# Layer norm's root taken for two tiles at once and applied behind the second product, w_out's mean from chunk sums, and one expert fewer turned by TensorE

## The chip, the core and the metric

The program runs on one core of a Trainium2 chip. Its time is device microseconds (us) of one execution. The kernel before takes 569.43 us as the median of 3 runs (568.84 to 570.12); the execution that the profiler recorded took 570.03 us, of which the trace spans 568.3.

## The reference

Three stages follow each other: a linear attention with a decaying state over 4 batches, 8 heads and 768 positions of width 48; a block with two products and a layer norm; and a mixture of 8 experts of which each token goes to one.

```python
h = x @ w_in                                    # 3072x384 @ 384x1024
e = exp(h - max(h)); sm = e / (sum(e) + 1e-9)
solu = h * sm
ln = (solu - mean(solu)) / sqrt(var(solu) + 1e-6) * g_ln
x = ln @ w_out                                  # 1024x384
expert = argmax(x @ w_gate); g = max of softmax(x @ w_gate)
out = g * (relu(x @ w1[expert]) @ w2[expert])
```

## The kernel before

The 3072 tokens are 24 tiles of 128 rows. Every product of precision is made of three fp16 products (high by high, high by low, low by high halves of fp32 numbers).

**Attention**, for each tile i: `kpow`, `rev` and `ktrans` prepare keys and receptances, `scores` multiplies them, `causal` masks them, `ahi` and `alo` split them into fp16 halves, `attend` makes the output, and `update`, `advance` and `decay` move the state on. For the first `NU` tiles the bonus term is made on TensorE by four products of two columns (L489); for later tiles by `ruk`, `asum` and `aval` on GpSimd and VectorE.

**The block**, for each tile: `yhi`, `ylo` and a DMA transpose turn its rows, `mm1` is the first product (18 matmuls of 512 columns), `hmax` its row maximum, `hexp` the exponential, `hsolu` the product with its sum. `hvar` squares on ScalarE. `hse` and `hseed` then make one factor per row from the sum of exponentials and the variance: one small ScalarE step (L583) and five more (L600 to L608), of which the second, a power of -1/2, is GpSimd's. `zscale` and `zlo` scale the rows by this factor into an fp16 high and low half, `ztrans` turns both by a DMA transpose, and `mm2` is the second product (24 matmuls of 392 columns, 384 of output and 8 gate scores, since `w_gate` is folded into `w_out`). For the last two tiles TensorE turns the scaled rows (`zturn`). `choose`, `xrow`, `gexp`, `gate`, `rank`, `place` and `send` pick the expert and send the row to its place in DRAM.

**Preparing w_out** (L238 to L290): it is loaded in four pairs of 128-row chunks, scaled by `g_ln`, extended by the gate's eight columns (`wout_fold`, `wout_gate`) and then freed of its column mean: `wout_mean` (L274) makes the mean with one matmul for each of the eight chunks, `wout_centre` takes it off.

**The experts**: nine parts y (expert 0 in two). `gather` fetches the rows; they are turned either by TensorE (`etrans`, L929) or by two DMA transposes (`eturn`). `EM` is a mask of the parts from y = 2 on that TensorE turns: 60 stands for y = 2, 3, 4, 5. `emm1` and `emm2` are the products, `rhi` and `rlo` split what stands between them, `split` (L832) makes the halves of the weights.

**The order of the work** is made by a planner inside the kernel (`plan`, L1271): each step is an `op` with an engine, a cost and what it comes after, and a table of numbers `X` gives due times. It takes steps one by one and fixes the order of instructions on each engine. Steps marked `either` go to GpSimd or VectorE, as the planner sees fit. Where it sees TensorE idle it puts matmuls of ones that compute nothing (`keep`, L1264), outside of the planned stretch from `K0` to `K1`. Each engine works through its instructions in their order.

Of the kernel before, what the change touches and what calls it, by code (L numbers as in the profile page):

```python
# [17 lines left out]
ALU = mybir.AluOpType  # L18
# [28 lines left out]
SQK = 2.0 / (SZ * 32 * FF)  # L47
GSC = 1.0 / (SW * SZ)
# [4 lines left out]
def body(ctx, tc, rkvs, rs, flat, w, u, w_in, w_out, w1, w2, out):  # L53
# [48 lines left out]
    X = dict(GQ=-1854.59, XA=-53.96, CF=172.95, CT=-2317.0, NF=5, NE=5, EM=60, E2=0, NU=5, QD=3, pr=1, look=-1606.34,
             prod=-4519.04, square=861.08, PK=14, ET=-65.59, GG=-3164.81, SO=-11608.92, FL=-1060.46, OL=1, ybuf=10,
             tmp=1, rkv=3, rT=3, LAT=0.06, SELF=0.05, PRE=0.6, EPS=0.09, TA=340.17, TB=415.99, TM=318.03, NA=8, NB=9,
             M0=1321.55, W0=-891.53, TW=2430.46, W1=-4264.59, TV=-522.72, PF=964.9, PW=1670.76, F0=972.63, EL=3, e=3,
             S0=-214.25, P0=7.7, D0=2.0, L0=-5070.67, L1=1799.29, U0=478.97, KG=-3.83, PT=2, ZT=4046.59, F2=-3101.97,
             TE=22.51, GA=-3791.47, GW=-3748.66, GN=2103.67, DB=1.0, KS=1.22, RD=0.1, RP=0.2, K0=91.31, K1=927.65,
             xtrans=206.21, kev=-3325.25, ahi=-5711.54, vlo=-3049.91, ruk=7806.69, attend=988.22, choose=10050.87,
             xhi=-4754.85, vhi=6188.75, own=7638.3, hvar=1885.43, hmax=-10736.42, gexp=6290.26, ktrans=-11388.48,
             ldr=3880.33, hexp=-1616.58, ztrans=1589.84, asum=8759.56, rev=-3492.12, xlo=239.09, decay=2965.24,  # L110
             alo=6303.56, rank=-1150.26, ld=125.71, xrow=13548.5, mm2=1284.96, causal=596.44, hseed=-5672.49,
             send=-7316.86, hsolu=3051.8, yout=-2009.24, zlo=3420.27, scores=-2533.28, place=-5242.89, WQ=-8553.91,
             advance=2287.51, update=-6787.84, zscale=-1258.1, hroot=-2799.46, mm1=-125.41, aval=6068.5, kpow=-2190.79)
# [19 lines left out]
    g2, low, chk = (const.tile([P, x], F32, name=n) for n, x in (("g2", NG + 6), ("low", NG + 7), ("chk", NCHK)))  # L133
# [71 lines left out]
    raw = {}  # L205

# [89 lines left out]
    def fold_all():  # L296
# [6 lines left out]
        for c in range(0, KF, 2):  # L303
# [7 lines left out]
            wout_gate(c)  # L311
        wout_mean()
# [260 lines left out]
    def hexp(i):  # L573
# [5 lines left out]
        A.activation(e, tk["h", i], AF.Exp, bias=st[:, 0:1], scale=1.0 if i is None else 1.0 / (SY * SI), accum_out=st[:, 1:2])  # L579
# [5 lines left out]
    def hsolu(i):  # L585
# [219 lines left out]
    def stem(key):  # L805
        return stem(key[0]) if isinstance(key, tuple) else key
# [758 lines left out]
```

## Time and profile before

| | |
|---|---|
| median of 3 runs | 569.43 us |
| profiled execution, its span | 570.03 us, 568.3 us |
| TensorE matmul busy | 531.8 us (94%) |
| VectorE busy | 415.3 us (73%) |
| ScalarE busy | 415.7 us (73%) |
| GpSimd busy | 243.1 us (43%) |

Attention and the block run side by side up to about 290 us; the block ends and the experts begin between about 320 and 360 us; the experts run to 554.9 us, and the last rows are written behind that. Shares of busy time are averages over stretches with different limits: a reader should look at the stretch that a change falls in, at whom the engine that sets the pace waits for there, and only then at the cost of one instruction. A matmul of fp32 stands in the trace as two rows.

### The profile page before, as it was taken

To read this page: it belongs to the slowest core of one execution; us is meant where nothing else is said; L and a number is where in the kernel's file an instruction comes from. 1 tells how busy PE (TensorE), PEld (TensorE's weight loads), DVE (VectorE), ACT (ScalarE), POOL (GpSimd) and SP (SyncE) were. 2 spreads that over 40 slices of the span, in tenths; PEclk is the share of its full clock that TensorE was granted. 3 is DMA by queue.
4 is the path that set the end of the run, shared out by engine and by line. 5 is a ranking of instruction groups with operands and counts; after the bars stand their busy time and mean duration, and the time that the engine had idled before them with its cause. 6 is when DMAs were issued, how large, how long until landed. Compare 5 with 4: busy or idle time off the path is not lost.

```text
span 568.3 us, 10629 instructions
## 1 busy us (share of the span) xinstructions
PE 531.8 (94%) x3892; PEld 352.0 (62%) x3892; DVE 415.3 (73%) x667; ACT 415.7 (73%) x898; POOL 243.1 (43%) x250
## 2 busy tenths in 40 slices
PE   3889999999999999999899988999999899999990
PEld 2777675666756676667555556864555455566770
DVE  7998979988779998899868617556777767755110
ACT  4868799998878687868658954988686969687210
POOL 4246733787878788968413131100023303040310
PEclk9999999999999999999899999999999999999995
DMA  7666691685967697742578426666469889882100
GB/s 285 207 191 196 188 254 58 135 180 123 163 184 143 157 196 144 192 122 64 103 190 177 103 70 215 187 191 212 163 166 233 211 215 213 193 246 85 27 24 25
DMA packets 113260, 91.38 MB, mean 161 GB/s; under 512 B 89148, under 2 KB 99350, under 8 KB 112816
## 3 DMA queue, kind: packets, MB, share of 16 engines
q1 hardware_dynamic: 108240, 81.14, 56.2%
q0 software_dynamic: 4960, 9.49, 5.5%
q8 instruction: 32, 0.52, 0.4%
q14 instruction: 28, 0.23, 0.1%
HBM read 57.19 MB, written 12.55 MB: 123 GB/s over the span
## 4 chain that ended last, share of the span: by engine, by line
PE 61%; DVE 16%; DMA 11%; ACT 7%; issue 3%; SPq 1%; POOL 0%; ACTq 0%; DVEq 0%; POOLq 0%
PE emm L949 13%; PE mm L650 10%; PE mm L565 10%; PE emm L992 8%; PE emm L974 7%; DMA xg<-xs 3%; DMA stage<-in_moe_w 3%; PE attend L493 2%; PE scores L459 2%; DMA raw<-in_moe_w_out 2%; PE update L507 2%; PE attend L496 2%; DVE z L615 2%; DVE e L588 1%; PE ktrans L443 1%
## 5 line engine op out<-in xcount | busy, mean ns | idle before, releaser
L1024 POOL DMA_INDIRECT out<-o,gt x29 | 35.1, 1211 | 175.1 <-ACT o L1020 96.2
L650 PE MATMUL mm<-wo,zT 128*128 128x392 f16 x576 | 101.2, 333 | 2.2 <-ACT zT L635 1.1
L949 PE MATMUL emm<-exT,w1h 128*128 128x256 f16 (+8 forms) x432 | 98.7, 317 | 2.5 <-DVE hl L963 2.5
L565 PE MATMUL mm<-wi,xT 128*128 128x512 f16 x432 | 97.2, 379 | 0.3 <-DMA xT<-yy 0.3
L650 PEld LDWEIGHTS <-zT 128*128 128x128 f16 x576 | 55.4, 99 | 40.9 <-issue 1.9
L565 PEld LDWEIGHTS <-xT 128*128 128x128 f16 x432 | 41.3, 98 | 47.5 <-DMA xT<-yy 0.5
L949 PE MATMUL emm<-exT,w1l 128*128 128x256 f16 (+8 forms) x216 | 68.5, 317 | 0.0
L949 PEld LDWEIGHTS <-w1h 128*128 128x128 f16 x432 | 41.7, 97 | 27.3 <-issue 2.9
L963 DVE SCALAR_TENSOR_TENSOR hl<-emm,hh 128x928 f16<-128x928 f32 (+8 forms) x32 | 32.2, 1008 | 30.3 <-ACT hh L960 30.2
L960 ACT ACTIVATE hh<-emm 128x928 f16<-128x928 f32 (+8 forms) x32 | 27.1, 846 | 30.9 <-PE emm L949 14.2
L446 POOL TENSOR_TENSOR rT<-rT,trT 128x512 f32<-128x512 f32 x21 | 30.2, 1441 | 33.5 <-DMA rT<-in_rT 27.9
L841 DVE SCALAR_TENSOR_TENSOR w1l<-stage,w1h 128x1024 f16<-128x1024 f32 x24 | 29.2, 1221 | 18.2 <-ACT w1h L837 17.9
L701 POOL DMA_INDIRECT xs<-row,pos x24 | 28.1, 1172 | 21.7 <-DMA xg<-xs 5.7
L615 DVE SCALAR_TENSOR_TENSOR z<-e,st,z 128x1024 f16<-128x1024 f32 x22 | 34.1, 1551 | 2.1 <-ACT z L611 2.1
L841 DVE SCALAR_TENSOR_TENSOR w2l<-stage,w2h 128x768 f16<-128x768 f32 x32 | 30.0, 951 | 7.5 <-ACT w2h L837 7.2
L571 DVE TENSOR_REDUCE st<-mm 128x1 f32<-128x1024 f32 x24 | 29.2, 1217 | 8.4 <-issue 4.1
L974 PE MATMUL emm<-w2h,hl 128*128 128x384 f16 (+3 forms) x104 | 33.9, 326 | 0.0
L974 PE MATMUL emm<-w2h,hh 128*128 128x384 f16 (+3 forms) x104 | 33.9, 326 | 0.0
L493 PE MATMUL attend<-sdec,rT 128*128 128x96 f32 x160 | 33.9, 296 | 0.0
L974 PE MATMUL emm<-w2l,hh 128*128 128x384 f16 (+3 forms) x104 | 33.9, 326 | 0.0
L992 PE MATMUL emm<-hl,w2h 128*128 128x464 f16 (+3 forms) x96 | 33.0, 344 | 0.0
L992 PE MATMUL emm<-hh,w2l 128*128 128x464 f16 (+3 forms) x96 | 33.0, 344 | 0.0
(256 smaller groups left out, 1357.6 us busy)
## 6 DMA issues: line engine op xcount, KB each, us to landing
rkv<-in_rkv SPq DMA_DIRECT2D x24, 576.0 KB
stage<-in_moe_w SPq DMA_DIRECT2D x16, 768.0 KB
stage<-in_moe_w SPq DMA_DIRECT2D x8, 1024.0 KB
rT<-in_rT SPq DMA_DIRECT2D x24, 256.0 KB
stage<-in_moe_w SPq DMA_DIRECT2D x8, 512.0 KB
raw<-in_moe_w_in SPq DMA_DIRECT2D x3, 1024.0 KB
raw<-in_moe_w_out SPq DMA_DIRECT2D x4, 768.0 KB
xs<-zf SPq DMA_DIRECT2D x8, 337.8 KB
```

The lines of the kernel that those rows point to most:

```text
L446: on[0].tensor_tensor(tk["rT", i], tk["rT", i], trT, op=ALU.mult)
L493: T.matmul(ps[:, j * 96:j * 96 + 96], rT[:, j, :], sdec[:, j].rearrange("p a d -> p (a d)"), start=True, stop=False, skip_group_check=True)
L565: T.matmul(ps[:, n, :], x[a][:, j, :], wi[b][:, j, n * 512:(n + 1) * 512], start=(j == 0 and m == 0), stop=(j == KD - 1 and m == 2))
L571: V.tensor_reduce(st[:, 0:1], tk["h", i], op=ALU.max, axis=AX.X, negate=True)
L615: V.scalar_tensor_tensor(z[:, 1, :], tk.pop(("e", i)), tk["st", i][:, 10:11], z[:, 0, :], op0=ALU.mult, op1=ALU.subtract)
L650: T.matmul(ps[:, 0:OW], zz[:, a, c, :], wo[b][:, c, :], start=(c == 0 and m == 0), stop=(c == KF - 1 and m == 2))
L841: V.scalar_tensor_tensor(lo, d[:, x], (S1, S2)[m - 1], hi, op0=ALU.mult, op1=ALU.subtract)
L949: T.matmul(ps[:, x, :].rearrange("p (j t) -> p j t", t=d["n"]), a[:, j, fc * P:(fc + 1) * P], d["xT"][:, 0:d["nt"], b, j, 0:d["n"]], start ...
L963: V.scalar_tensor_tensor(cols(d, "hl", q), d.pop(("pm", q)), 0.0, cols(d, "hh", q), op0=ALU.max, op1=ALU.subtract)
L974: T.matmul(ps[0:n, 0:DM], a[:, c, j * n:j * n + n], b[:, c, :], start=(c == 0 and m == 0), stop=(c == KF - 1 and m == 2))
L992: T.matmul(ps[:, 0:d["nr"]], a[:, c, m * P:(m + 1) * P], b[:, c, :], start=(c == 0 and x == 0), stop=(c == KF - 1 and x == 2))
L1024: G.indirect_dma_start(out=apart["out"].pop(0), out_offset=bass.IndirectOffsetOnAxis(ap=d["gt"][0:n, j, 1:2].bitcast(U32), axis=0), in_=d. ...
```

## The change

The factor of layer norm is no longer applied to the rows before the second product. `zscale` and `zlo` now multiply by a constant `ZC`, directly behind `hsolu`; `mm2` works on rows without the root, and the root is applied to its results, as the scale of `xrow`, `choose` and `gexp`. `hse` and `hseed` go from the planned part; `hroot` stands in their place: seven small steps on columns of two tiles at once (one ScalarE, four VectorE, two GpSimd; the last two tiles get one each), 13 times in all. `choose` and `xrow` of both tiles of a pair come after it. The two tiles that TensorE turns are turned as they come from `hsolu`, and the constant is applied on the way out of PSUM.

`wosum` adds the pairs of w_out chunks (four pairs, three additions of 128x784 fp32, on GpSimd or VectorE), and the mean is made of the two sums by two matmuls in place of eight.

`EM` is 28 in place of 60: TensorE turns y = 2, 3, 4, and y = 5 goes to the DMA transposes. `NU` and `NE` are 4 in place of 5: tile 4 makes its bonus term on GpSimd and VectorE, and its `aval` and `decay` leave ScalarE. All due times of the table differ, and `K0` is 488 in place of 91, so that `keep` may stand anywhere in the planned program before that. `marks2` checks three more bounds.

```diff
-             tmp=1, rkv=3, rT=3, LAT=0.06, SELF=0.05, PRE=0.6, EPS=0.09, TA=340.17, TB=415.99, TM=318.03, NA=8, NB=9,
+             tmp=1, rkv=3, rT=3, LAT=0.06, SELF=0.05, PRE=0.6, EPS=0.13, TA=423.54, TB=347.88, TM=332.72, NA=8,
...
+    def wout_sum(c, eng=None):
+        (eng or on[0]).tensor_tensor(raw["sum"], raw["sum"] if c > 2 else sto[:, 0:2], sto[:, c:c + 2], op=ALU.add)
...
-        for c in range(KF):
-            T.matmul(ps[:, 0:OW], mmean.to_broadcast([P, P]), sto[:, c, :], start=(c == 0), stop=(c == KF - 1))
+        for c in range(2):
+            T.matmul(ps[:, 0:OW], mmean.to_broadcast([P, P]), raw["sum"][:, c, :], start=(c == 0), stop=(c == 1))
...
+    def hroot(p):
+
+        c = slice(2 * p, 2 * p + 2) if 2 * p < NT - 2 else slice(p + NT // 2 - 1, p + NT // 2)
+        s, m, v, t, y, f, nf = (lv[:, x, c] for x in range(7))
+        A.activation(t, s, AF.Square, scale=1e-3 * ZA, bias=zeps)
+        yield
+        V.scalar_tensor_tensor(t, v, ZA ** 2, t, op0=ALU.mult, op1=ALU.add)
+        yield
+        G.tensor_tensor(y, t, mhalf.to_broadcast([P, c.stop - c.start]), op=ALU.pow)
+        yield
+        G.tensor_tensor(f, y, y, op=ALU.mult)
+        yield
+        V.tensor_tensor(t, t, f, op=ALU.mult)
+        yield
+        V.scalar_tensor_tensor(nf, t, 3.0, y, op0=ALU.subtract, op1=ALU.mult)
+        yield
+        V.tensor_scalar(f, nf, -1.0, None, op0=ALU.mult)
...
-        A.activation(tk["z", i][:, 0, :], tk["e", i], AF.Copy, scale=tk["st", i][:, 10:11])
+        A.activation(ztile(i)[:, 0, :], tk["e", i], AF.Copy, scale=tk["st", i][:, 10:11] if i is None else ZC)
...
-        A.activation(row[:, 0:DM], tk["pz", i][:, 0:DM], AF.Copy, scale=GSC if i is not None else tk["scale"][:, 0:1])
+        A.activation(row[:, 0:DM], tk["pz", i][:, 0:DM], AF.Copy, scale=lv[:, 5, i:i + 1] if i is not None else tk["scale"][:, 0:1])
...
-        op(("hseed", i), "", [("act", .29), ("pool", .58), ("act", .3), ("act", .36), ("act", .3)], [("hvar", i), ("hse", i)], hseed, i, first=f + X["hseed"])
+            op(("hroot", p), "", [("act", .28), ("dve", .17), ("pool", .58), ("pool", .3), ("dve", .17), ("dve", .17), ("dve", .17)], [("hvar", i)] + [("hvar", i - 1)] * (i < NT - 2), hroot, p, first=f + X["hseed"])
```

On TensorE, around the mean of w_out, the order before has two `wout_fold`s apart, eight matmuls of the mean, and a first product behind them (`mm_925` and `mm_1041` are those of tiles 3 and 4):

```order
L565 MATMUL mm_925<-wi_112,xT 128x512
...
L259 MATMUL wout_part<-ident,sto 128x128 x6
L459 MATMUL scores<-rT_143,kT 128x128 x8
L269 MATMUL wout_fold<-few,gT 128x8 x6
L443 MATMUL ktrans<-ident,kp_137 128x128 x4
L278 MATMUL mean<-sto,mmean 128x392 x8
L565 LDWEIGHTS xT
L565 MATMUL mm_1041<-wi_111,xT 128x512
```

The same place now:

```order
L576 MATMUL mm_901<-wi_114,xT 128x512
...
L265 MATMUL wout_part<-ident,sto 128x128 x6
L275 MATMUL wout_fold<-few,gT 128x8 x12
L470 MATMUL scores<-rT_146,kT 128x128 x8
L454 MATMUL ktrans<-ident,kp_140 128x128 x4
L287 MATMUL mean<-sum,mmean 128x392 x2
L576 LDWEIGHTS xT
L576 MATMUL mm_1020<-wi_114,xT 128x512
```

The last folds stand ahead of the scores, and six matmuls of the mean are gone. Between this mean and the first `mm2`, the order before holds the first product of tile 4, the scores of tile 8, seven `keep` and the attention of tile 6; now it holds the first products of tiles 4 and 5, the attention of tiles 6 and 7 and the update of tile 7, and no `keep`.

On TensorE, where the block ends, the order before goes from the second product of tile 23 (`mm_4286`) straight to the turning of the first expert's rows:

```order
L650 LDWEIGHTS zT
L650 MATMUL mm_4286<-wo_113,zT 128x392
L929 MATMUL etrans<-ident,xg 128x128 x6
L684 LDWEIGHTS mask_77
L684 MATMUL rank<-oh,mask_77 128x8
L685 LDWEIGHTS ones_71
L685 MATMUL rank<-cum,ones_71 128x8
L949 LDWEIGHTS w1h
L949 MATMUL emm_4351<-exT,w1h 128x256
```

The same place now:

```order
L678 MATMUL mm_4184<-wo_116,zT 128x392
L712 LDWEIGHTS mask_77
L712 MATMUL rank<-oh,mask_77 128x8
L713 LDWEIGHTS ones_71
L713 MATMUL rank<-cum,ones_71 128x8
L1303 LDWEIGHTS ones_71
L1303 MATMUL keep<-ones_71 128x512
...
L957 MATMUL etrans<-ident,xg 128x128 x6
...
L977 LDWEIGHTS w1h
L977 MATMUL emm_4284<-exT,w1h 128x256
```

Two `keep` stand ahead of the turning and five behind it; twelve more follow ahead of y = 1 and y = 2. Of 43 `keep` in all, 19 stand here and 24 early; before, all 36 stood early.

On VectorE, late in the loop, the steps that make `choose` and the low half for a tile stand before without any step of the root:

```order
L663 MAX mx<-mm_3431 128x8
L670 TENSOR_SCALAR oh<-mm_3431,mx 128x8
L615 SCALAR_TENSOR_TENSOR z<-e,st,z 128x1024
L501 SCALAR_TENSOR_TENSOR av<-attend,av 128x384
L438 SCALAR_TENSOR_TENSOR vl<-rkv_141,vh 128x384
```

The like place now, with the root of tiles 16 and 17 (`lv`):

```order
L617 SCALAR_TENSOR_TENSOR lv<-lv 128x2
L698 TENSOR_SCALAR oh<-mm_3238,mx 128x8
L414 TENSOR_TENSOR kp_140<-rkv_143,tkm 128x8x48
L648 SCALAR_TENSOR_TENSOR z<-e,z 128x1024
L582 TENSOR_REDUCE st<-mm_3295 128x1
L623 TENSOR_TENSOR lv<-lv 128x2
L717 ISA mx,rs<-rank,oh 128x8
L717 ISA rs 128x1
L625 SCALAR_TENSOR_TENSOR lv<-lv 128x2
L627 TENSOR_SCALAR lv<-lv 128x2
```

Between the root's first step on VectorE and its second, in which GpSimd's two fall, four other instructions stand.

## Rows read from the trace of the kernel before

**Rows 1.** Busy time by stretch: length, engines (instructions), granted clock, DMA share, GB/s.
```profile
20.00:60.00 40.00, 38.01 (x306) 31.64 (x306) 37.62 (x50) 31.79 (x81) 19.70 (x15) 0.96 0.60 185
...
200.00:250.00 50.00, 49.40 (x444) 33.90 (x444) 45.43 (x68) 39.19 (x99) 42.18 (x39) 1.00 0.74 164
250.00:300.00 50.00, 47.88 (x390) 30.80 (x390) 41.97 (x66) 34.33 (x87) 25.67 (x25) 0.97 0.50 124
...
450.00:500.00 50.00, 50.00 (x299) 28.91 (x297) 36.41 (x43) 37.06 (x58) 6.24 (x6) 1.00 0.88 214
```

**Rows 2.** Waits of TensorE: whom for, us in total, times, longest.
```profile
PE scores L459 <- ACT kT L450: 4.7, 3, 2.3
PE emm L949 <- DVE hl L963: 2.5, 2, 1.6
...
PE rank L684 <- DVE exT L935: 1.2, 1, 1.2
PE mm L650 <- ACT zT L635: 1.1, 1, 1.1
PE etrans L929 <- DMA xg<-xs: 1.0, 1, 1.0
PE mm L650 <- DVE zT L639: 0.8, 1, 0.8
```

**Rows 3.** Groups of TensorE by shape: count, busy us, mean ns, idle before.
```profile
L1269 PE MATMUL keep<-ones 128*128 128x512 f16 x36 | 10.1, 411 | 0.0
...
L278 PE MATMUL mean<-sto,mmean 128*128 128x392 f32 x16 | 5.4, 492 | 0.0
...
L489 PE MATMUL attend<-uw,pr 128*128 128x2 f32 x40 | 4.9, 245 | 0.0
...
L929 PE MATMUL etrans<-ident,xg 100*128 100x100 f32 x12 | 1.5, 261 | 0.2 <-PE etrans L929 0.2
```

**Rows 4.** TensorE in order of time behind the mean: start, us, count.
```profile
94.04 1.69 PE L1269 MATMUL keep<-ones 128*128 128x512 f16 x7
```

**Rows 5.** TensorE in order of time, end of attention: start, us, count, idle before.
```profile
263.83 4.15 PE L650 MATMUL mm<-wo,zT 128*128 128x392 f16 x24
...
272.18 1.16 PE L459 MATMUL scores<-rT,kT 64*128 64x128 f32 x16 [2.12 <-ACT kT L450]
...
273.34 5.82 PE L650 MATMUL mm<-wo,zT 128*128 128x392 f16 x24
```

**Rows 6.** Groups of ScalarE by shape: small steps of the factor.
```profile
L606 ACT ACTIVATE st<-st,mthree 128x1 f32<-128x1 f32 x24 | 9.1, 377 | 0.1
L604 ACT ACTIVATE st<-st 128x1 f32<-128x1 f32 x24 | 6.9, 289 | 4.0 <-POOL st L602 3.6
...
L583 ACT ACTIVATE st<-st,seps 128x1 f32<-128x1 f32 x24 | 6.7, 285 | 0.1
```

**Rows 7.** Groups of VectorE by shape.
```profile
L615 DVE SCALAR_TENSOR_TENSOR z<-e,st,z 128x1024 f16<-128x1024 f32 x22 | 34.1, 1551 | 2.1 <-ACT z L611 2.1
...
L475 DVE TENSOR_TENSOR al<-AT,ah 128x1024 f16<-128x1024 f32 x8 | 14.2, 1772 | 2.5 <-ACT ah L471 2.5
...
L282 DVE TENSOR_TENSOR sto<-mean,sto 128x784 f32<-128x784 f32 x4 | 3.7, 966 | 1.1 <-PE mean L278 1.1
...
L344 DVE TENSOR_TENSOR tt<-tt 128x4 f32<-128x4 f32 x6 | 1.0, 167 | 0.2
```

**Rows 8.** Groups of GpSimd by shape.
```profile
L475 POOL TENSOR_TENSOR al<-AT,ah 128x1024 f16<-128x1024 f32 x11 | 24.1, 2190 | 6.0 <-ACT ah L471 5.8
...
L602 POOL TENSOR_TENSOR st<-st,mhalf 128x1 f32<-128x1 f32 x24 | 18.7, 779 | 32.7 <-ACT st L600 32.7
```

**Rows 9.** GpSimd and VectorE at 68 us, and VectorE at 79, in order of time.
```profile
67.90 2.13 POOL L475 TENSOR_TENSOR al<-AT,ah 128x1024 f16<-128x1024 f32 x1 [0.37 <-ACT ah L471]
...
67.95 2.50 DVE L534 SCALAR_TENSOR_TENSOR yy<-av,yy 128x384 f16<-128x384 f32 x1
...
78.64 0.55 DVE L534 SCALAR_TENSOR_TENSOR yy<-av,yy 128x384 f16<-128x384 f32 x1
```

More of the change, by code (lines that the diff above doesn't have):

```diff
@@ L100, in body @@
+    for t, x in ((mhalf, -0.5), (mthree, -3.0), (seps, 1e-12 * SQK), (zeps, 1e-12 * ZA), (geps, 1e-9 * SX * S1 * S2), (mmean, -1.0 / FF)):
         V.memset(t, x)
-    X = dict(GQ=-1854.59, XA=-53.96, CF=172.95, CT=-2317.0, NF=5, NE=5, EM=60, E2=0, NU=5, QD=3, pr=1, look=-1606.34,
-             prod=-4519.04, square=861.08, PK=14, ET=-65.59, GG=-3164.81, SO=-11608.92, FL=-1060.46, OL=1, ybuf=10,
-             tmp=1, rkv=3, rT=3, LAT=0.06, SELF=0.05, PRE=0.6, EPS=0.09, TA=340.17, TB=415.99, TM=318.03, NA=8, NB=9,
[L105 to L113, printed above, removed]
@@ new lines, in body @@
+    X = dict(wosum=-1635.67, GQ=-616.8, XA=1394.41, CF=-290.97, CT=-6359.1, NF=5, NE=4, EM=28, E2=0, NU=4, QD=3, pr=1,
+             look=-2341.52, prod=-6524.65, square=2604.7, PK=14, ET=528.66, GG=-3384.61, SO=-18943.02, FL=-798.97, OL=1,
+             ybuf=10, tmp=1, rkv=3, rT=3, LAT=0.06, SELF=0.05, PRE=0.6, EPS=0.13, TA=423.54, TB=347.88, TM=332.72, NA=8,
+             NB=9, M0=845.85, W0=-2374.1, TW=2832.34, W1=-4662.95, TV=-874.11, PF=-1936.1, PW=4107.56, F0=1220.97, EL=3,
+             e=3, S0=-1054.86, P0=7.7, D0=2.0, L0=-6821.53, L1=5887.81, U0=-1599.74, KG=-8.84, PT=2, ZT=820.97,
+             F2=-3035.94, TE=132.85, GA=-5551.93, GW=-3010.05, GN=7245.56, DB=1.13, KS=1.34, RD=0.1, RP=0.2, K0=488.46,
+             K1=1255.14, xtrans=-2101.6, kev=-5486.82, ahi=-6274.18, vlo=779.5, ruk=17058.24, attend=940.63,
+             choose=11798.2, xhi=-6359.67, vhi=3018.11, own=6575.55, hvar=3502.44, hmax=-16082.56, gexp=7779.16,
+             ktrans=-8999.85, ldr=1692.18, hexp=2493.89, ztrans=-1764.42, asum=2142.54, rev=-3671.2, xlo=1537.36,
+             decay=4482.54, alo=6355.85, rank=1187.18, ld=-663.05, xrow=9507.73, mm2=1410.61, causal=926.75,
+             hseed=-12404.97, send=-11051.31, hsolu=2227.53, yout=1363.01, zlo=8166.78, scores=-1290.24, place=-8047.87,
+             WQ=-4668.31, advance=500.44, update=-7582.49, zscale=-5085.08, hroot=490.76, mm1=111.97, aval=14450.14,
+             kpow=-530.85)
@@ L126, in fold_pools @@
         sto = cv.tile([P, KF, OW], F32, name="sto", bufs=1)
+        raw["sum"] = cv.tile([P, 2, OW], F32, name="sum", bufs=1)
         return cv, sto
@@ L132, in body @@
     hacc = const.tile([P, 4 * (E + 1)], F32, name="hacc")
-    g2, low, chk = (const.tile([P, x], F32, name=n) for n, x in (("g2", NG + 6), ("low", NG + 7), ("chk", NCHK)))
+    lv = const.tile([P, 7, NT], F32, name="lv")
+    g2, low, chk = (const.tile([P, x], F32, name=n) for n, x in (("g2", NG + 6), ("low", NG + 10), ("chk", NCHK)))
     G.memset(hacc, 0.0)
@@ L1157, in body @@
         op(("send", i), "", [("act", .2), ("pool", 1.1), ("none", 4.0)], [("place", i), ("xrow", i), ("gate", i)] + [("fill", e) for e in range(E)], send, i, first=f + X["send"])
+    for i in range(NT):
+        for n in ("choose", "xrow"):
+            ops[n, i]["after"].append(("hroot", i // 2 if i < NT - 2 else i - NT // 2 + 1))
     b_left = set(ops)
```

69 lines of the change are left out of this document (37 added, 32 removed).

## The prediction

> **What bounds the kernel now.** I read the busy time by stretch first. TensorE has 49.40 us of 50 busy in the loop from 200 us on, and all 50.00 of 50 in the experts from 450 us on [rows 1]. The granted clock stands at 1.00 there, so this is work at the full 2.4 GHz and not slow work. In such stretches a matmul that goes is time that goes. Between 20 and 60 us it is different: TensorE's 38.01 of 40 contain most of the 36 `keep` matmuls, 10.1 us in all [rows 3], which compute nothing; VectorE is at 37.62 of 40 with real work and sets the pace [rows 1].
>
> The second view is whom TensorE waits for. Beyond the start it waits little: 4.7 us for ScalarE's `kT`, 2.5 us for VectorE's `hl` in the experts, and where the block ends 1.2, 1.1, 1.0 and 0.8 us, together 4.1 [rows 2]. The third is order of time: of the waits for `kT` one stands at 272 us. It is 2.12 us, and behind it a second product takes 5.82 us in place of 4.15 [rows 5]: TensorE had stood idle, and its clock then fell to the lower level, 1.2 GHz, for a while (0.97 is the granted mean from 250 to 300 us [rows 1]). That is 1.67 us more, 3.8 us for this one stall.
>
> So time can come from four places: TensorE's own work, the stall at 272 us, the waits where the block ends, and the pace of VectorE at the start.
>
> **The change part by part.** I add to the profiled execution's own time, 570.03 us, of which 568.3 is span and 1.73 lies around it; it is 0.60 above the median of the runs.
>
> *The mean of w_out.* Eight fp32 matmuls are 16 rows and 5.4 us; two are four rows. Twelve rows at 5.4/16 = 0.34 go: -4.0 us of TensorE [rows 3]. Three additions of 128x784 come: two on GpSimd and one on VectorE. A like addition on VectorE takes 0.966 [rows 7]; on GpSimd the nearest is the 128x1024 subtract of 2.19 [rows 8], and I take 2 each. The last one stands between the last `wout_fold` and the mean. It is covered by the scores and `ktrans` that the order now puts there, and by VectorE, which has five operations to do before it can take the mean off; uncovered it would cost its 2 us.
>
> *Tile 4's bonus term.* Four products of two columns go, 8 of 40 rows in 4.9 us: -1.0 us [rows 3].
>
> *What the start takes back.* These 5.0 us go where VectorE sets the pace. If it alone decided when `mm2` may begin, all 5.0 would come back as waiting; if not, none. VectorE does not get less to do there: it loses two preparations of tile 1 and the bonus of tile 4, and gains an addition, four small root steps and an earlier `zlo`. But the order brings work forward: before the first `mm2` it now has a first product, an attention and an update more and no `keep`, where seven `keep` of 1.69 us stood [rows 4]. That work would otherwise stand in the full stretch behind, so the saving is kept if TensorE is fed. I take +1.0, nearer to the end of nothing lost.
>
> *The factor.* Per tile ScalarE loses five small steps, four of 285 to 289 ns and one of 377, about 1.52 us [rows 6], 36.6 in all, and gets one step per root. TensorE does not see this in full stretches: ScalarE is not the bound there (39.19 of 50 [rows 1]). It does matter at 272 us, where `kT` came late from ScalarE. Fewer steps in front of it make that wait shorter; but it was late because VectorE was, and VectorE has no less to do. The ends are 0 and -3.8 (wait and slow clock gone); I take -1.5.
>
> VectorE gets four root steps in each of 13 roots at about 0.167 [rows 7]: 8.7 us. Five of the `alo` subtracts (1.772 each [rows 7], 8.9 us) go from VectorE to GpSimd. By count the two cancel. The root's steps on VectorE wait for GpSimd's power (0.779 [rows 8]) and its square, and in order behind the waiting step stand `place`, the next `hmax` and `hsolu`, for which the first product's PSUM bank and then `mm2` wait. Four other instructions stand between, the low half and a row maximum among them, longer than power and square together. So 0; without this cover each root could hold VectorE for those two and a subtract in front of them on GpSimd (the rival below).
>
> `choose` and `xrow` now wait for the root of the pair, so the first tile of a pair keeps its PSUM bank about a tile longer. Behind `xrow` on ScalarE stand the gate's steps and the next exponential. The order puts the root's ScalarE step ahead of them, and nobody needs the sent row before the gather: 0. It could cost a wait for a bank; I see none from this in the trace of before and put its worst into the range.
>
> *The moved subtracts.* A subtract on GpSimd is not free for VectorE. At 67.95 us a split of 384 columns took 2.50 us beside a GpSimd subtract of 2.13 that had begun 0.05 earlier; at 79 us the same shape took 0.55 [rows 9]. So five moved subtracts give VectorE between 8.9 us (nothing beside them suffers) and -0.9 us (each holds up such a split by 1.95). The Trainium skill, "SBUF — State Buffer", section "Who interferes with whom", says that VectorE instructions with two SBUF inputs and GpSimd instructions that read SBUF lock each other out for a whole instruction; this row agrees. By that rule the relief of VectorE is nearer to the second end, and the sum stays as it is, since TensorE is the bound, but the slower rival gets nearer.
>
> *Expert part y = 5.* Twelve transposes of 100 columns go from TensorE: -1.5 us [rows 3], in a stretch where it has 50.00 of 50. Two DMA transposes come, in SP's queue ahead of the last two loads of expert 4's weights, with the share of the DMA engines at most 0.88 [rows 1]. Those weights are needed two products of other rows later, so 0; if the queue ran late, TensorE would wait for them. The orders of the products differ there too; the 2.5 us of waits for `hl` may go or double, and I take 0.
>
> *Where the block ends.* The waits of 4.1 us come from the last two tiles' long way through factor, scaling and turning, and from the gathers. That way is shorter by the factor and one scaling pass. But 19 `keep` stand here now, and they run whether the wait is there or not: 19 x 1.69/7 = 4.6 us [rows 4]. Best case they just fill what was waiting, +0.5; worst they come on top, +4.6. I take +1.0.
>
> *The three checks* stand ahead of the last products on a VectorE with nothing else to do: 0.
>
> Sum: -4.0 - 1.0 + 1.0 - 1.5 - 1.5 + 1.0 = -6.0, so 564.0 for a profiled execution like that of before, and 563.4 from the median of 569.43. I forecast 563.8.
>
> **The rivals.**
>
> *More is gained.* The stall at 272 us goes wholly (-3.8 in place of -1.5), the waits for `hl` go (-2.5), and the start takes nothing back (-1.0): 563.8 - 5.8 = 558.0. For it: ScalarE is relieved by 33 us, and the loop's full stretches leave it idle. Against it: VectorE was at the root of the stall.
>
> *The start eats its savings.* VectorE sets the pace to the mean and beyond, the 5.0 us come back as waits, the stall stays: 570.03 - 1.5 + 1.0 = 569.5, no change. For it: 37.62 of 40 [rows 1]. Against it: the work that is brought forward.
>
> *VectorE becomes the bound of the loop (slower).* Its idle time is 4.6 us of 50 at 200 us [rows 1]. Two roots fall into 50 us. Each could hold it for a subtract, a power and a square on GpSimd, at most 2.19 + 0.78 + 0.78 = 3.75, so 7.5, and 1.3 for their own steps. The moved subtracts give back at most 8.9 over some 190 us of loop, 2.3 per 50. That is 7.5 + 1.3 - 2.3 - 4.6 = 1.9 lost per 50 us, 7.2 over 190. The savings inside this part are then no savings, only the 1.5 of the experts remain: 570.03 + 7.2 - 1.5 = 575.7. It decides from the point where a root holds VectorE for (4.6 + 2.3 - 1.3)/2 = 2.8 us; if the moved subtracts give nothing back, from 1.65. Against it: the four instructions in between.
>
> *The `keep` are pure cost.* The waits at the block's end stay and 4.6 us come on top: 563.8 + 3.6 = 567.4.
>
> **How the numbers follow.** The forecast (561 to 567) gets 0.48, more gained 0.15, the start eats its savings 0.12, VectorE the bound 0.15, `keep` pure cost 0.10. A change under 0.2% of 569.43, 1.1 us, is about what a measurement of this kernel can't tell from none. Faster: 0.48 + 0.15, most of the 0.10, and a little of the third case, 0.72. Same: most of the third, 0.11. Slower: 0.17, the fourth with a tail of waits for banks and weights. The range is to leave out 2 in 10: from 558.0, the better case, to 571.5, which is past the third case and reaches into the slower one. The forecast's own range is 561 to 567.
>
> **What would show it right or wrong.** Right: four rows of the mean, about 1.3 us; the first `mm2` at most 2 us later than before, with a first product and an attention more in front of it; no wait of 2 us for `kT`; `etrans` without the 100-column shape; idle time of TensorE at the block's end under 2 us with 19 `keep` in it. Wrong: a wait of TensorE for the mean or for `wo`; VectorE idle before L623 for POOL by more than 1.65 us a root; TensorE's share in the loop below 98%; a gap before expert 4's second product for its weights.

## The result, and the profile after

The changed kernel takes 562.66 us (median of 4 runs, 561.07 to 562.90) beside 569.36 of the kernel before: ratio 0.9881, 95% interval 0.9841 to 0.9922. Measured once more beside the kernel before (e5 below) it was 0.9843 (0.9795 to 0.9892). So it is faster, by 6.7 us in the first pair of medians; the forecast was 563.8. Some executions of a kernel run some per cent longer at a lower granted clock: the ratios here leave them out, the medians and single runs given below do not. The execution of the profile took 562.63 us with a span of 560.9, 7.4 less than before.

| stage of the profile, us | before | after | difference |
|---|---|---|---|
| up to the first `mm2` | 96.54 | 97.00 | +0.46 |
| first `mm2` to the end of the last | 243.13 | 235.99 | -7.14 |
| to the first expert product | 2.11 | 2.37 | +0.26 |
| expert products | 212.96 | 212.19 | -0.77 |
| rest | 13.56 | 13.35 | -0.21 |

The busy times of three of these stages follow, in the columns of [rows 1]: the stage, its length, then TensorE's busy time. Before:

```profile
0.00:96.54 96.54, 83.60 (x655) 63.22 (x656) 85.30 (x140) 75.81 (x168) 46.20 (x63) 0.98 0.64 194
96.54:339.67 243.13, 237.84 (x1929) 154.43 (x1924) 200.44 (x317) 189.40 (x486) 156.97 (x154) 0.99 0.65 146
...
341.78:554.74 212.96, 209.32 (x1311) 133.64 (x1310) 127.50 (x199) 147.78 (x239) 37.86 (x31) 1.00 0.62 173
```

After:

```profile
0.00:97.00 97.00, 85.35 (x664) 64.04 (x665) 86.90 (x145) 74.22 (x150) 56.99 (x71) 0.95 0.70 208
97.00:332.99 235.99, 231.11 (x1887) 151.09 (x1884) 206.38 (x355) 170.58 (x385) 163.11 (x160) 1.00 0.64 144
...
335.36:547.55 212.19, 210.82 (x1311) 133.60 (x1310) 128.71 (x204) 148.27 (x238) 40.40 (x31) 1.00 0.64 177
```

Up to the end of the last `mm2`, TensorE is busy 5.0 us less (321.44 to 316.46) and idle 1.7 us less (18.23 to 16.53). The gain shows behind the first `mm2`, but most of the work that went stood in front of it. Now one more first product (18 matmuls) and one more attention and update stand there (and the scores of one tile fewer), and the first `mm2` is only 0.46 late. By groups the 5.0 us are: the mean -2.5, tile 4's bonus -1.0, twelve `keep` fewer at the start -1.9 (24 in 8.2 us for 36 in 10.1), a second product that ran at the lower clock before -1.7, and rows beside the mean that ran at the lower clock after, +1.8; the rest is small. In the experts idle time fell by 2.3 us and busy time rose by 1.5: twelve `keep` now stand there, and the transposes of y = 5 went.

The waits of TensorE after, to be read beside [rows 2] (whom for, us in total, times, longest):

```profile
PE scores L470 <- ACT kT L461: 3.4, 3, 1.6
PE ktrans L454 <- DVE mx L691: 1.1, 1, 1.1
PE etrans L957 <- ACT o L1008: 1.1, 3, 0.5
PE count L748 <- POOL cum L720: 1.0, 1, 1.0
...
PE emm L977 <- DVE hl L991: 0.3, 1, 0.3
```

The waits of `mm2` for `zT` are gone, those for `hl` fell from 2.5 to 0.3, and new ones of about 1 us came: for VectorE's `mx` and GpSimd's `cum`. The groups that answer to [rows 3]:

```profile
L1303 PE MATMUL keep<-ones 128*128 128x512 f16 x43 | 13.3, 434 | 0.0
...
L500 PE MATMUL attend<-uw,pr 128*128 128x2 f32 x32 | 3.9, 243 | 0.0
...
L287 PE MATMUL mean<-sum,mmean 128*128 128x392 f32 x4 | 2.9, 876 | 0.0
```

The mean has four rows, as said, but one takes 876 ns where it took 492. TensorE in order of time around it shows why (start, us):

```profile
77.25 2.93 PE L275 MATMUL wout_fold<-few,gT 128*128 128x8 f32 x24
80.11 2.08 PE L470 MATMUL scores<-rT,kT 64*128 64x128 f32 x16
82.12 1.11 PE L454 MATMUL ktrans<-ident,kp 128*128 128x128 f32 x4
83.03 2.88 PE L287 MATMUL mean<-sum,mmean 128*128 128x392 f32 x4
85.71 4.44 PE L576 MATMUL mm<-wi,xT 128*128 128x512 f16 x18
```

Behind 24 rows of 8 columns the scores take 2.08 us; elsewhere the same 16 rows take 1.16. The mean granted clock from 60 to 100 us is 0.91, where it was 1.00 before; so for some us it was the lower level, 1.2 GHz. The wait of 2.12 us in [rows 5] stands at the scores of tile 23. There it is gone; the longest wait for `kT` in the loop is now at tile 21:

```profile
251.96 1.16 PE L470 MATMUL scores<-rT,kT 64*128 64x128 f32 x16 [1.64 <-ACT kT L461]
253.06 4.15 PE L678 MATMUL mm<-wo,zT 128*128 128x392 f16 x24
```

It is 1.64 us, and the second product behind it takes 4.15 us and not 5.82: the clock stayed up. At both places ScalarE was not busy with small steps before it made `kT`. It stood idle and waited for VectorE, first before, then after:

```profile
271.15 0.49 ACT L655 ACTIVATE row<-mm 128x384 f32<-128x384 f32 x1 [2.76 <-DVE oh L670]
```

```profile
250.37 1.06 ACT L482 ACTIVATE ah<-AT 128x1024 f16<-128x1024 f32 x1 [2.67 <-DVE AT L478]
```

In both cases `kT` is ScalarE's next instruction.

VectorE's root steps are dearer than the 0.167 us taken from [rows 7]:

```profile
L617 DVE SCALAR_TENSOR_TENSOR lv<-lv 128x2 f32<-128x2 f32 x11 | 4.6, 420 | 0.2 <-ACT lv L615 0.2
...
L623 DVE TENSOR_TENSOR lv<-lv 128x2 f32<-128x2 f32 x11 | 4.2, 381 | 1.3 <-POOL lv L621 1.3
...
L627 DVE TENSOR_SCALAR lv<-lv 128x2 f32<-128x2 f32 x11 | 3.4, 307 | 0.3
L625 DVE SCALAR_TENSOR_TENSOR lv<-lv 128x2 f32<-128x2 f32 x11 | 3.2, 287 | 0.3
```

### The profile page after: what moved, and what is told of

It is laid out like the page before. It is cut to its first block, busy times and chain, and to the rows that moved or that the text cites. A ratio compares the mean times of both kernels' runs of the same rounds, so it can differ in the third digit from the quotient of the medians.

```text
span 560.9 us, 10536 instructions
## 1 busy us (share of the span) xinstructions
PE 529.7 (94%) x3867; PEld 350.1 (62%) x3867; DVE 424.2 (76%) x718; ACT 396.0 (71%) x780; POOL 263.2 (47%) x265
## 4 chain that ended last, share of the span: by engine, by line
PE 68%; DVE 13%; ACT 6%; DMA 5%; issue 5%; POOL 1%; SPq 0%; ACTq 0%; DVEq 0%; POOLq 0%
PE emm L977 16%; PE mm L678 12%; PE mm L576 11%; PE emm L1020 8%; PE emm L1002 7%; PE scores L470 3%; PE attend L504 2%; PE attend L507 2%; PE update L518 2%; DMA rkv<-in_rkv 2%; DVE yy L545 1%; DMA stage<-in_moe_w 1%; DMA xg<-xs 1%; DMA raw<-in_moe_w_out 1%; DVE vl L449 1%
## 5 line engine op out<-in xcount | busy, mean ns | idle before, releaser
L1052 POOL DMA_INDIRECT out<-o,gt x29 | 37.7, 1299 | 171.6 <-ACT o L1048 97.4
L678 PE MATMUL mm<-wo,zT 128*128 128x392 f16 x576 | 99.3, 329 | 0.5 <-ACT kT L461 0.5
L486 POOL TENSOR_TENSOR al<-AT,ah 128x1024 f16<-128x1024 f32 x16 | 37.0, 2311 | 7.1 <-ACT ah L482 6.9
L457 POOL TENSOR_TENSOR rT<-rT,trT 128x512 f32<-128x512 f32 x21 | 28.6, 1362 | 21.0 <-DMA rT<-in_rT 16.5
L414 POOL TENSOR_TENSOR kp<-rkv,tkm 128x384 f32<-128x384 f32 x23 | 25.1, 1093 | 18.7 <-DMA rkv<-in_rkv 14.8
L648 DVE SCALAR_TENSOR_TENSOR z<-e,z 128x1024 f16<-128x1024 f32 x22 | 33.2, 1509 | 0.3 <-ACT z L609 0.3
L470 PE MATMUL scores<-rT,kT 64*128 64x128 f32 x384 | 29.4, 296 | 4.2 <-ACT kT L461 3.4
```

The costliest lines, as they stand in the source:

```text
L470: T.matmul(ps[:, a, j * P:(j + 1) * P], kT[h, j, :], rT[h, j, :], start=True, stop=True)
L486: on[0].tensor_tensor(al, tk.pop(("at", i)), tk["ah", i], op=ALU.subtract)
L648: V.scalar_tensor_tensor(z[:, 1, :], tk.pop(("e", i)), tk["st", i][:, 10:11] if i is None else ZC, z[:, 0, :], op0=ALU.mult, op1=ALU.subtract)
L678: T.matmul(ps[:, 0:OW], zz[:, a, c, :], wo[b][:, c, :], start=(c == 0 and m == 0), stop=(c == KF - 1 and m == 2))
L1052: G.indirect_dma_start(out=apart["out"].pop(0), out_offset=bass.IndirectOffsetOnAxis(ap=d["gt"][0:n, j, 1:2].bitcast(U32), axis=0), in_=d. ...
```

## The experiments

All are compared with the kernel before on the chip of their own runs. Its medians there were 569.59 us (e1 to e4), 571.84 (e5 to e8) and 571.13 (e9 to e12), its single runs 565 to 581, and the intervals are some 0.3 to 0.7% to either side. The changed kernel itself stands at 0.988 and 0.984; an edit of it is judged against these two. It ran on the chip of e6 and e7, and not on those of e1 to e4 and e9 to e12. "Same order" means that the planner's numbers are left alone, so the instructions keep their places.

**e5, the changed kernel again.** No edit.

> The changed kernel itself once more, beside the kernel before on the chip of these runs, as the measure for the kernels that differ from it by one edit. Expected ratio to the kernel before 0.988, within the interval of the first measurement, some 563. If the clock falls at chance places from run to run, the single runs spread over some us, and a profile can show the lower clock in another place than at 78 to 86 us.

0.9843 (0.9795 to 0.9892), 562.33 us, runs from 561.41 to 563.74. Its span of 559.7 has the slow stretch too, in part: scores 2.08, but the mean 1.60, and the first `mm2` at 95.26. So the same instructions meet the lower clock for a longer or shorter time from one execution to the next.

**e1, keep the clock up before the mean.**

```diff
         ps = gTs[c] = sml("wout_fold", slot)
+        if c == KF - 2:
+            for _ in range(7):
+                T.matmul(ps, ones16, ones16.unsqueeze(1).to_broadcast([P, 4, P]), start=True, stop=True)
```

> The changed kernel, in the same order, with seven keep matmuls (128x512) put between the third and the fourth group of wout_fold, where 24 matmuls of 8 columns stand one behind the other and behind which the scores, ktrans, the mean and a first product ran at the lower clock. Theory (TensorE sets the time here, and the changed kernel lost part of the mean's saving to the lower clock): scores 2.08 to 1.16, ktrans 1.11 to 0.62, mean 2.88 to about 1.4, mm1 4.44 to 4.05, together -3.3 us, for 7 x 0.21 = 1.5 us of keep: 1 to 2 us faster than the changed kernel, some 561.0. Rival (VectorE sets the pace up to the first second product, so what TensorE saves comes back as waiting): no gain, up to 1.5 us slower, 562.7 to 564.2.

0.9903 (0.9869 to 0.9937), 565.02 us: not faster than the changed kernel. Where it was aimed it worked: the profile has scores 1.16, `ktrans` 0.65, mean 1.58, first product 4.05, though the mean waited 0.58 us for GpSimd's sum. The execution of the profile (568.78 us, longer than the median) lost time elsewhere: the first product at 67.87 us took 6.75 us in place of 4.04. That product stands ahead of the seven `keep`, so they can't have caused it. It took 5.11 us in e2, whose edit comes behind it too, and 4.04 in e3: here again the clock differs from one execution to the next. Why the time gained at 80 us doesn't show in the median is open.

**e7, both places, and the last addition on VectorE.** As e1, with five `keep` in front of the second group as well, and

```diff
-        (eng or on[0]).tensor_tensor(raw["sum"], ...
+        (V if c == KF - 2 else eng or on[0]).tensor_tensor(raw["sum"], ...
```

> The changed kernel, in the same order, with keep matmuls in front of two groups of wout_fold (5 before the second, 7 before the last) and the last of the three additions on VectorE in place of GpSimd. Theory: the lower clock between 63 and 87 us (3.1 us lost in the changed kernel's profile) goes, the 1.15 us in which the mean waited for GpSimd's sum where the clock was up goes, 12 keep cost 2.6 less what they fill of the waiting at 67 us (0.6): net -1 to -2.5 against the changed kernel, some 561. Rival (the keep take as much as the clock gives back, VectorE has the addition's 1.0 us on its path): 0 to +1.5.

0.9908 (0.9867 to 0.9950), 568.11 us: slower than the changed kernel on the same chip, for its shortest run (564.18) is longer than the longest of e5 (563.74). Up to the first `mm2` the theory holds: clock 1.00 from 20 to 100 us, and that product at 94.26 in place of 95.26 in e5. Between first and last `mm2` it loses 5.7 us (241.66 in place of 236.00). One place shows some 3 us of it. GpSimd in order of time, then TensorE:

```profile
266.89 0.99 POOL L421 TENSOR_TENSOR ru<-rkv,ub 128x384 f32<-128x384 f32 x1 [2.67 <-DMA rkv<-in_rkv]
267.85 0.19 POOL L723 TENSOR_TENSOR cum<-cum,oh 128x8 f16<-128x8 f16 x1
```

```profile
268.09 0.17 PE L751 MATMUL count<-cum,ones 128*128 128x8 f16 x1 [2.27 <-POOL cum L723]
268.12 5.82 PE L681 MATMUL mm<-wo,zT 128*128 128x392 f16 x24
```

GpSimd waits for a load of `rkv`; behind this wait stands `cum`, for `cum` TensorE waits 2.27 us, and the second product behind it runs partly at the lower clock, 5.82 us as once in [rows 5]. In the first profile of the changed kernel GpSimd waits 1.18 us for that load and goes on at 265.63, TensorE waits 0.96, and the product takes 4.14. So the microsecond gained at the start meets a load that isn't earlier, and it is lost there. That the clock fell too may be this execution's chance (see e12); the other 2.7 us are not explained.

**e2, the mean from eight chunks again, same order.**

```diff
-        for c in range(2):
-            T.matmul(ps[:, 0:OW], ..., raw["sum"][:, c, :], start=(c == 0), stop=(c == 1))
+        for c in range(KF):
+            T.matmul(ps[:, 0:OW], ..., sto[:, c, :], start=(c == 0), stop=(c == KF - 1))
```

> The changed kernel, in the same order, with the mean taken again from the eight chunks (16 rows) in the place where the four rows stand; the three additions stay and nobody reads them. Theory (the rows of the mean are full time of TensorE): 12 rows more, +4.1 us at the upper clock, up to +8 if the clock stays low; if the 16 rows bring the clock back earlier, part of the 3 us of slow clock is saved: +3 to +5, some 566.5. Rival (the start is paced by VectorE, TensorE's savings there come back as waits): at most +1, 563.7.

0.9993 (0.9957 to 1.0030): the gain is gone, 1.1 to 1.5% against the changed kernel, 6 to 9 us and so more than the 4 us of the rows. The profile has the mean at 5.43 us, scores at 1.16, the first `mm2` at 98.64, and 238.69 us from there to the last. These last 2.7 us more lie where no instruction was changed; whether the later start makes them, the run does not show.

**e11, the mean alone, in the kernel before and its order.** Two matmuls for eight, and three additions on VectorE behind `wout_gate`.

> The kernel before, in its own order, with the mean from the sums of chunks alone (three additions on VectorE behind wout_gate, four rows in place of 16). Theory (full time of TensorE, the prediction's first term): the mean takes 1.4 in place of 5.4, the first second product comes 2 to 4 us earlier, and the time falls by as much: 566 to 568. Rival (VectorE, with 2.9 us more work, sets the pace up to the first second product): the first second product comes when it came, 0 to +1.

1.0062 (1.0032 to 1.0092), 572.40 us: slower. The four rows save nothing there:

```profile
86.90 2.95 PE L281 MATMUL mean<-sum,mmean 128*128 128x392 f32 x4 [1.39 <-DVE sum L275]
89.64 4.36 PE L568 MATMUL mm<-wi,xT 128*128 128x512 f16 x18
...
95.02 1.69 PE L1272 MATMUL keep<-ones 128*128 128x512 f16 x7
...
98.54 1.65 PE L653 MATMUL mm<-wo,zT 128*128 128x392 f16 x9
```

TensorE waits 1.39 us for the third addition, the four rows and the product behind run partly at the lower clock, the seven `keep` stand where they stood, and the first `mm2` is 2.0 us later than before. The rest has the old length (243.32 from first to last `mm2`). So VectorE's additions stood in the way here, in an order that was not made for them.

**e3, without the 19 `keep` from the block's end on, same order.**

```diff
+        kept[0] += n
+        if kept[0] > 24:
+            return
```

> The changed kernel, in the same order, without the 19 keep matmuls from the end of the block on. Theory (they fill times in which TensorE would wait for the gathered rows): 0 to -1 us, 561.7 to 562.7, with idle time of TensorE in their place. Rival 1 (they are pure cost): -4.6 us, 558.1. Rival 2 (they hold the clock up for the first expert products): without them the granted clock falls there and it is 1 to 3 us slower.

0.9978 (0.9951 to 1.0006): 1.0 to 1.4% slower than the changed kernel. They are no cost. Its stages, where the second row is first to last `mm2` and the last the expert products:

```profile
0.00:94.39 94.39, 81.06 (x664) 61.54 (x665) 87.82 (x144) 74.39 (x150) 59.29 (x71) 1.00 0.75 213
94.39:330.48 236.09, 231.17 (x1887) 151.12 (x1884) 206.84 (x356) 170.34 (x385) 163.94 (x161) 1.00 0.64 144
...
332.85:550.37 217.52, 210.17 (x1299) 132.88 (x1298) 128.70 (x204) 147.94 (x238) 40.85 (x31) 0.99 0.64 173
```

The expert part is 5.3 us longer: idle 7.35 us in place of 1.37, and from 345 to 350 us the granted clock was 0.74. TensorE waited there for VectorE's `hl` (3.5 us), ScalarE's `o` (1.9) and `hh` (1.8), and not for a load. Waits for `hl` of that size also stand in e9 and e10 below, where all `keep` are in place, and this execution began its experts 2.5 us earlier; how much of the 5.3 us the `keep` were worth the run does not part. It has a second use: up to 332 us it is the changed kernel unaltered, and here the clock did not fall:

```profile
76.44 2.74 PE L275 MATMUL wout_fold<-few,gT 128*128 128x8 f32 x24
79.11 1.16 PE L470 MATMUL scores<-rT,kT 64*128 64x128 f32 x16
...
82.06 1.58 PE L287 MATMUL mean<-sum,mmean 128*128 128x392 f32 x4 [1.15 <-POOL sum L281]
```

The mean's rows take 1.58, but now TensorE waits 1.15 us for GpSimd's addition, which the slow clock had hidden in the first profile. The first `mm2` comes at 94.39, 2.6 us earlier.

**e4, five small ScalarE steps for each tile.** They stand behind each variance, have one column, and nobody reads them.

```diff
+            for _ in range(5):
+                A.activation(lv[:, 7, i:i + 1], lv[:, 0, i:i + 1], AF.Identity, scale=2.0, bias=zeps)
```

> The changed kernel, in the same order, with five small ScalarE steps (128x1, nobody reads them) behind each tile's variance, 24 x 5 x about 0.2 to 0.29 us, so ScalarE's load is about that of the kernel before. Theory (TensorE is the bound, ScalarE's relief is worth a stall or two): +0 to +4, my middle +1.5, 564.2, and the waits for kT grow. Rival (the gain came mainly from ScalarE's relief): +5 or more, 568.

1.0029 (0.9998 to 1.0060), 571.48 us: the whole gain is gone, some 1.5 to 1.9%. From first to last `mm2` it is 245.76 us in place of 235.99, TensorE nearly as busy as in the changed kernel (232.79, there 231.11) and idle for 13.0 us in place of 4.9. The steps added, and the waits, many and small:

```profile
L612 ACT ACTIVATE lv<-lv,zeps 128x1 f32<-128x1 f32 x120 | 35.0, 291 | 3.1
```


```profile
PE scores L470 <- ACT kT L461: 2.6, 4, 1.1
PE rank L716 <- POOL cum L723: 2.2, 1, 2.2
PE ktrans L454 <- POOL kp L414: 1.9, 2, 1.0
PE mm L576 <- DVE AT L478: 1.5, 1, 1.5
PE mm L681 <- ACT kT L461: 1.3, 1, 1.3
```

The two longest waits for `kT`, 1.3 and 1.1 us, stand behind five of the added steps (1.6 us) in ScalarE's queue. But the load is now more than the change took away: ScalarE is busy for 425.9 us here, 415.7 in the kernel before and 396.0 in the changed one.

**e12, two of ScalarE's steps taken out of the kernel before**, in its own order (the refined power is left out, the factor is -2 times the power).

```diff
-        A.activation(q, t, AF.Copy, scale=y)
-        yield
-        A.activation(g, q, AF.Identity, scale=y, bias=mthree)
-        yield
-        A.activation(f, g, AF.Copy, scale=y)
+        A.activation(f, y, AF.Copy, scale=-2.0)
```

> The kernel before, in its own order, with two of ScalarE's five small steps of the factor per tile left out (the two that refine the power, so the factor is the unrefined power): 24 x 2 x 0.285 = 13.7 us less for ScalarE and the factor 0.6 us earlier, TensorE's work the same. Theory 1 (the prediction's term for the factor, -1.5 for 36.6 us): 0 to -1, 569. Theory 2 (the small steps stand on the path in the loop, since five added ones cost the changed kernel 9 us): -2 to -4, 566.

1.0001 (0.9970 to 1.0033): no gain. From first to last `mm2` it is 240.24 us, 2.9 less than before; but the first `mm2` came 1.05 later and the experts took 1.4 longer, and the sum is nothing. The place of [rows 5]:

```profile
272.59 1.16 PE L459 MATMUL scores<-rT,kT 64*128 64x128 f32 x16 [2.12 <-ACT kT L450]
273.75 4.14 PE L646 MATMUL mm<-wo,zT 128*128 128x392 f16 x24
```

The wait for `kT` is the same 2.12 us: fewer steps on ScalarE did not shorten it. But the product behind it took 4.14 us and not 5.82, so the clock fell behind this wait in one execution and not in another, and 1.7 of the 2.9 us are that. With the old order the relief of ScalarE alone isn't worth what its loss costs in the new one. e8 was the same with a third step gone, which makes a term under the root out of the sum of exponentials. Without that term the execution went through the kernel's slow path (1656 us), and its time tells nothing here; the wait for `kT` at that place was 2.28 us in it.

> The kernel before, in its own order, with three of ScalarE's five small steps of the factor per tile left out (the scaled square of the sum and the two steps that refine the power; so the factor is the unrefined power without its small constant term): 24 x 3 x about 0.285 = 20.5 us less for ScalarE, TensorE's work the same. Theory 1 (TensorE is the bound; the prediction's term for the factor, -1.5): 0 to -2, some 568. Theory 2 (five added steps cost the changed kernel some 8 us, so ScalarE's small steps stand on the path in the loop): -3 to -5, some 565.

**e6, GpSimd's power three times over.**

```diff
+        for _ in range(2):
+            G.tensor_tensor(y, t, mhalf.to_broadcast([P, c.stop - c.start]), op=ALU.pow)
```

> The changed kernel, in the same order, in which GpSimd takes the power of each of the 13 roots three times (the same values again), about 2 x 0.6 to 1.1 us more for each root, 16 to 29 us of GpSimd in all. Theory (VectorE's root steps have enough other work in front of them, the root's path has slack): 0 to +2, some 564. Rival of the prediction (VectorE is held by each root and is the bound of the loop): +1.2 to 2.2 per root over 10 roots of the loop, +10 or more, 574.

1.0187 (1.0120 to 1.0254), 584.39 us: 22 us slower than the changed kernel. VectorE's waits name the place; L623 is the square on GpSimd in this kernel, L625 the step behind it:

```profile
DVE lv L625 <- POOL lv L623: 14.0, 11, 2.4
```

14.0 us in 11 waits, 1.3 us each; in the changed kernel it was 2.3 us in 3. From first to last `mm2` 17.7 us are added, of which TensorE is busy for 7.2, at a granted clock of 0.97.

**e10, the root's last three VectorE steps on GpSimd.**

```diff
-        V.tensor_tensor(t, t, f, op=ALU.mult)
...
-        V.scalar_tensor_tensor(nf, t, 3.0, y, op0=ALU.subtract, op1=ALU.mult)
...
-        V.tensor_scalar(f, nf, -1.0, None, op0=ALU.mult)
+        G.tensor_tensor(t, t, f, op=ALU.mult)
+        G.tensor_tensor(t, t, mthree.to_broadcast([P, n]), op=ALU.add)
+        G.tensor_tensor(nf, t, y, op=ALU.mult)
+        G.tensor_tensor(f, nf, mone.to_broadcast([P, n]), op=ALU.mult)
```

> The changed kernel, in the same order, with the last three of the root's four VectorE steps taken by GpSimd (as four steps of two columns there), so that VectorE no longer waits for GpSimd in a root. Theory (VectorE is at its limit in the loop: its three steps take 4.2 + 3.4 + 3.2 us and wait 2.3 us in the changed kernel, and 1.3 us more of waiting per root cost 22 us): 2 to 4 faster, 559. Rival 1 (GpSimd's subtracts and the root itself come later and the order doesn't fit any more): 2 to 6 slower. Rival 2 (VectorE has slack): the same, 562.

0.9914 (0.9877 to 0.9952), 565.86 us: no version that beats the changed kernel. From first to last `mm2` it takes 238.10, 2.1 more than in the changed kernel, and in the experts 215.76, 3.6 more; the first `mm2` is 1.1 earlier.

**e9, a mere shift.** Two `keep` ahead of the first group of `wout_fold`.

> The changed kernel, in the same order, with two keep matmuls (0.43 us) in front of the first group of wout_fold at 56 us and nothing else. It measures how much a mere shift moves. Theory 1 (the terms add up, a shift costs what it takes): 0 to +0.5, 562.8, ratio to the kernel before 0.985. Theory 2 (the order's places were fitted to the chip, and a shift of any kind brings waits and falls of the clock elsewhere; each edit so far in this order came out 2 to 9 us slower): +3 to +5, 566, and then the same-order edits show their own size only less these 3 to 5 us.

0.9934 (0.9894 to 0.9973), 566.51 us, single runs from 560.96 to 569.34. The loop did not mind: first to last `mm2` takes 236.45. What was lost stands in the experts, 215.98 us in place of 212.19, with waits for `hl`:

```profile
PE emm L980 <- DVE hl L994: 2.7, 5, 1.3
```

e10, on the same chip, has 2.6 us of waits for `hl` and 215.76. Whether the shift or that chip makes these waits is open, since the unaltered changed kernel was not run there. So of e9's 4 us I can't say that a shift costs them (its interval also overlaps that of the first pair, 0.9841 to 0.9922); of e10's loss about 3.5 us are of this unsettled kind too.

## Why the prediction was right, and where it was not

The forecast was -6.0 for the profiled execution and -5.6 for the median; -7.4 and -6.7 came. Its direction and place hold: work leaves TensorE at the start, work is brought forward into the space, and the waits at the block's end go. Of the terms several were missed, and that the misses cancel is in part luck: the lower clock took 1.8 us at the start of the first profile and cost 1.7 at the stall in the profile before, and both come and go from one execution to the next.

- *The mean, -4.0.* Four rows, as said. In the profile they saved 2.5 us (5.4 to 2.9) and the clock took back 1.8 beside them (scores 0.92, `ktrans` 0.49, first product 0.39). With the clock up (e3) the rows save 3.85 and 1.15 of waiting for the third addition comes. I had called that addition covered: wrong, it was covered only by slow rows. e2 shows that the new order loses its gain without it, by more than its rows; e11 that it is worth nothing in the old one.
- *The bonus of tile 4, -1.0.* 4.9 to 3.9.
- *What the start takes back, +1.0.* The first `mm2` is 0.46 late with the extra work in front of it. The rival in which the start eats its savings did not come here. It came in e11, where the old order has `keep` and no work to bring forward. Twelve early `keep` fewer, 1.9 us, had no term in the sum.
- *The factor, -1.5.* The number is near what came and the mechanism is not. In the profiled pair the longest wait in the loop is 0.5 us shorter and the clock cost of 1.67 is gone, together 2.2; new waits for `mx`, `cum` and `kp` took 2.5 in the same stage. But in e12, with two of ScalarE's steps out of each tile, the wait is 2.12 us as before, and the clock cost is gone all the same. ScalarE stood idle ahead of `kT` and waited for VectorE; the prediction said that VectorE was the reason and still took -1.5 for fewer steps. So fewer steps did not take the wait away from tile 23; that leaves the changed order as a whole, and the 1.67 comes and goes with the execution. Nor is ScalarE relieved by the 33 us counted: its busy time fell by 19.7 (415.7 to 396.0), among other reasons because three instructions of each tile that now take the root as their scale grew longer (last section). "TensorE does not see this in full stretches" is too strong: e4, with 35.0 us of small steps added, cost the whole gain, and has TensorE waiting for a `kT` that stands behind them. From a busy share of 39 in 50 I had concluded that ScalarE sets nothing. What the relief is worth in the changed kernel is not shown: e4 loads ScalarE by 10 us more than the kernel before, and e12 gained nothing.
- *The root on VectorE, 0.* The cover of four instructions held (2.3 us of waits in 13 roots), and TensorE's share of the stage is 97.9% (231.11 of 235.99), 97.8 before; "below 98%" was no sign of being wrong, as the kernel before was there already. The count of 8.7 us was wrong: the 11 pairs alone took 15.4, and with the five subtracts gone VectorE is still 8.9 us busier (415.3 to 424.2). The slower rival was nearer than its limits said: in e6, with 1.3 us of wait for each root, less than the 1.65 from which the prediction let it decide, the kernel is slower than before. What VectorE's wait does there and what GpSimd's own delay (16 us more busy) adds is not parted.
- *Part y = 5, -1.5.* The 100-column shape is gone, and no gap stood before expert 4's weights. The expert part gained 0.8: the transposes' 1.5 and 2.2 us of waits for `hl`, less 12 `keep` of about 0.24. It was not tried alone.
- *The block's end, +1.0.* From the last `mm2` to the first expert product it is +0.26. Idle time from 320 to 360 us fell from 4.42 to 0.70 us. `keep` as pure cost is refuted by e3, which is slower without them.
- *The checks, 0.* The rest took 13.35 in place of 13.56.

*More gained* (558.0) did not come, though two of its three conditions did (the waits for `hl`, the start); the clock at 80 us and the new small waits took their place. Not settled: what each part is worth by itself. No edit in the changed kernel's order came out faster; the ratios lie 0.2 to 3.5% higher, the smallest of these differences (e1) within the noise, and e3 and e10 too, which take work from TensorE and from VectorE, did not gain. By e2 and e11 the terms don't add up: the same edit is worth more than its rows in one order and nothing in the other.

## What to carry to other kernels

Work taken off the engine that sets the pace is worth what the order puts into its place: an order that brought a first product forward lost its gain without the two-matmul mean (e2), and one that kept its filler got slower with it (e11). A busy share of 78% does not make an engine's small steps free (e4), and taking steps off an engine does not shorten a wait in front of which that engine stood idle (e12): look at what the late instruction itself waited for. Count a small step on VectorE beside a busy GpSimd at a mean measured there (0.42 us for L617), not at the duration of an undisturbed one (0.15).

## What the hardware showed that was not expected

VectorE steps of two columns took as long as wide ones where GpSimd was at work. GpSimd in order of time at one root, and then VectorE:

```profile
188.12 2.13 POOL L486 TENSOR_TENSOR al<-AT,ah 128x1024 f16<-128x1024 f32 x1
...
190.36 0.99 POOL L414 TENSOR_TENSOR kp<-rkv,tkm 128x384 f32<-128x384 f32 x1
```

```profile
189.16 1.10 DVE L623 TENSOR_TENSOR lv<-lv 128x2 f32<-128x2 f32 x1
190.29 0.16 DVE L625 SCALAR_TENSOR_TENSOR lv<-lv 128x2 f32<-128x2 f32 x1
190.49 0.89 DVE L627 TENSOR_SCALAR lv<-lv 128x2 f32<-128x2 f32 x1
```

L623 ends as `al` ends (190.26 and 190.25), L627 as `kp` ends (191.38 and 191.35). Undisturbed these steps take 0.14 to 0.17 us. The Trainium skill, "SBUF — State Buffer", section "Who interferes with whom", has the first case: a VectorE instruction with two SBUF inputs contends with a GpSimd instruction that reads SBUF. L627 is a `tensor_scalar` with one SBUF input, which by the same section does not contend outside of the two-port modes but can be in one of them; whether it ran in one no run here shows. That it waited for `kp` is read from the ends of the two rows.

The clock fell behind sparse work or a wait in some executions and not in others of the same instructions: the 16 rows of scores behind the folds took 2.08 us in the first profile and in e5 and 1.16 in e3, and the first `mm2` came at 97.00, 95.26 and 94.39. Behind the same wait of 2.12 us a second product took 5.82 us in the kernel before and 4.14 in e12.

A scale that ScalarE reads from a column took about 0.09 us longer than a constant one. The row of `xrow`, before with a constant and after with the root as its scale:

```profile
L655 ACT ACTIVATE row<-mm 128x384 f32<-128x384 f32 x24 | 11.5, 479 | 8.9 <-DVE oh L670 2.8 <-DVE mx L663 2.4 <-PE count L720 1.7
```

```profile
L683 ACT ACTIVATE row<-mm,lv 128x384 f32<-128x384 f32 x24 | 13.7, 574 | 9.4 <-PE mm L678 4.6 <-PE rank L713 2.5 <-issue 1.4
```

The small steps of `choose` and `gexp` went from 193 to 284 ns and from 257 to 356; the three together are 6.7 us over 24 tiles. `zscale`, which went the other way, fell from 1143 to 1051.
